# Where two centring products and one evacuation stand in the opening of a layernorm, attention and SwiGLU kernel

## The chip, the cores and the metric

The kernel runs on one core of one Trainium2 chip. The metric is the device time of one execution in microseconds (us), lower is better. Before the change three runs gave 814.28, 814.46 and 814.59 us, with a median of 814.46 us.

## What is computed

The input x has 2048 rows of 1024 values. Each row is normalised, and the normalised rows feed two branches whose results are joined:

```python
xn = _layernorm(x, axis=-1)          # (x - mean) / sqrt(var + eps)
s  = _A_ref(xn, A_wqkv, A_wo)        # 32 heads, window 8, dilation 2, then @ wo
g  = _silu(_B_ref(xn, B_w1, B_w3, B_w2))   # (silu(xn@w1) * (xn@w3)) @ w2
return x + s * g
```

For the change only the opening matters: the mean and the deviation of the first rows of x, and the products of those rows with the q and k parts of wqkv.

## The kernel before, in words

The 2048 rows are worked through in four chunks of 512 rows. For each chunk TensorE computes q, k and v (`qkv`), 14 blocks of gate and up products (`up_block`), the down projection in two halves (`down_half`) and the output projection (`wo_proj`). VectorE's attention work is slipped in beside it by a planner (`Side`) with hand-set costs and due times. Outside the planner the order on every engine is the order in which the code is written: the kernel switches the scheduler off (`tc.manual_schedule()`, line 98). The framework puts in the semaphores for data and for buffers that are used again.

Chunk 0 has no earlier work to hide its layernorm behind, so its opening is written out by hand (lines 511 to 697). Its 512 rows are four tiles of 128 rows, tiles 0 to 3. Tiles 0 and 1 (256 rows, `HC`) go first and by a detour:

- `raw_transpose` (L562) turns the raw tile with TensorE into PSUM, in two banks of four 128x128 blocks each: `b0[0]`, `b0[1]` for tile 0 and `b1[0]`, `b1[1]` for tile 1. The first bank of a tile holds blocks kt 0 to 3 of the 1024 columns, the second kt 4 to 7.
- The row sums become diagonal matrices: `dgs[0]` (L593) from tile 0's sum, and `dgs[1]` from tile 1's two half sums (L594, then L595). `center` (L568) adds a product of ones and this diagonal to a bank, which takes the mean from every row.
- `copy_in` (L574) brings a centred bank to SBUF, into `xcT[:, kt, rows]`, by ScalarE for tile 0 and VectorE for tile 1.
- The products of q and k (`part`, L620) run on `xcT`, centred but not scaled. The factor 1/deviation comes later: `R` holds it (L643, L648, L654), and VectorE multiplies by it on the way out (L291).

After the copies the code issues the statistics of tiles 0 and 1: on ScalarE the squares (L553, L554, L557) and two roots (`std`, L544), on VectorE `stats(1)` (L206 twice, L541), `recip(0, 2)` (L547) and `norm0(0)`, `norm0(1)` (L209). These lines stand ahead of the first `part` call in the code.

The q products go to eight accumulators `banks[0]` to `banks[7]`, one for each column group j, first tile rows 0 to 255. `part(t, kt, js, a, b, ...)` issues one product for each j in `js`, of block kt with columns a to b of the rows. The order is: kt 0 with j 0 to 3 on tile 0 alone (L637), the same on tile 1 (L638), kt 0 with j 4 to 6 on both (L639), kt 1 with j 0 to 6 (L640), then in the loop L641 j = 7 for kt 0 and kt 1, and all eight j for kt 2 to 7.

PSUM has the pools `psum_mm` with six buffers and `psum_aux` with two, one bank each. `psum_aux` first holds `b0[0]` and `b0[1]`, later `banks[4]` and `banks[6]`. `psum_mm` first holds the warm-up target `wps`, `b1[0]` and `b1[1]`, which leaves three free buffers, and later the other six accumulators. `busy(n, w)` (L520) issues n products on constants into `wps`, whose result is not read.

The weights come through SyncE's queue: after four half tiles of x, eight transfers of 256 KB bring the q part of wqkv, one for each kt (L138), then the k part follows with tiles 2 and 3 of x between (L157).

Of the kernel before, what the change touches and what calls it, by code (L numbers as in the profile page):

```python
# [45 lines left out]
def kernel(  # L46
# [12 lines left out]
    P = 128  # L59
# [455 lines left out]
    def one(n):  # L515
        return nc.const_aps.tensor(1.0, (P, n), BF16)

    def busy(n, w=CH):
        for _ in range(n):
            nc.tensor.matmul(wps[:, 0:w], lhsT=one(P), rhs=one(w), start=True, stop=True)  # L520

    V, A = nc.vector.tensor_copy, nc.scalar.copy
# [44 lines left out]
    def center(bank, st, i0=0, n=4):  # L567
        nc.tensor.matmul(  # L568
            bank[:, i0:i0 + n, :], lhsT=ones_b[:], rhs=dgs[st][:].unsqueeze(1).to_broadcast([P, n, P]),
            start=False, stop=True, skip_group_check=True,  # L570
        )

    def copy_in(src, st, k0, n, eng):
        eng(out=xcT[:, k0:k0 + n, st * P:(st + 1) * P], in_=src)  # L574

    b0 = [psum_aux.tile([P, 4, P], FP32, tag="aux", name=f"xt0_{h}") for h in range(2)]
    b1 = [psum_mm.tile([P, 4, P], FP32, tag="mm", name=f"xt1_{h}") for h in range(2)]
# [18 lines left out]
        out=dgs[1][:], in0=ident_d[:], scalar=half1[:, 1:2], in1=dga[:], op0=ALU.mult, op1=ALU.add,  # L596
    )
    center(b0[0], 0)
    busy(2, P)
    center(b1[0], 1, 0, 2)  # L600
    center(b1[0], 1, 2, 2)
    center(b0[1], 0)
    center(b1[1], 1)
    copy_in(b0[0][:, 0:2, :], 0, 0, 2, A)
    copy_in(b0[0][:, 2:4, :], 0, 2, 2, A)
    copy_in(b1[0][:, 0:2, :], 1, 0, 2, V)
    copy_in(b1[0][:, 2:4, :], 1, 2, 2, V)
    copy_in(b0[1][:], 0, 4, 4, A)
    copy_in(b1[1][:], 1, 4, 4, V)

    wq, wk = take_q(0), take_q(1)
    banks = [psum_mm.tile([P, CH], FP32, tag="mm", name="ps_qkv") for _ in range(6)]
# [3 lines left out]
    def part(t, kt, js, a, b, first, src):  # L616

        for j in js:
            o = t * HC + a % HC
            nc.tensor.matmul(  # L620
                banks[j][:, o:o + b - a], lhsT=(wq, wk)[t](kt, j), rhs=src[:, kt, a:b],
                start=first, stop=(kt == KT - 1), skip_group_check=True,
            )
# [9 lines left out]
    for i in range(3):  # L633
        nc.gpsimd.tensor_copy(out=rsb[:, i, :], in_=rs0[:, 0:2] if i == 0 else rest[:])
        if i < 2:
            nc.gpsimd.tensor_sub(rest[:], rs0[:, 0:2] if i == 0 else rest[:], rsb[:, i, :])
    part(0, 0, range(4), 0, P, True, xcT)  # L637
    part(0, 0, range(4), P, HC, False, xcT)  # L638
    part(0, 0, range(4, NJ - 1), 0, HC, True, xcT)  # L639
    part(0, 1, range(NJ - 1), 0, HC, False, xcT)  # L640
# [126 lines left out]
```

## Time and profile before

| What | Value |
|---|---|
| median of three runs | 814.46 us |
| the profiled execution, its own time | 814.30 us |
| span of the profiled execution | 812.5 us |
| TensorE (PE) busy | 804.0 us, 99% of the span |
| VectorE (DVE) busy | 474.7 us, 58% |
| ScalarE (ACT) busy | 188.3 us, 23% |
| GpSimd (POOL) busy | 95.9 us, 12% |
| mean DMA rate over the span | 181 GB/s |
| DMA rate from 6.30 to 10.09 us | 365 GB/s |
| chain that ended last | PE 97% |

All times inside the execution count from the span's start. PE is the matmul side of TensorE and PEld its weight loads, which run beside the matmuls. A timeline row gives start, length, engine, line, operation, output <- inputs, shapes, the number of instructions merged into it, and in brackets the idle time ahead of it with what ended that idle time. [...]

### The profile page before, as it was taken

The numbers are of one execution on the slowest core, as the hardware profiler recorded it, in microseconds if no ns is written. First come the engines' busy times: TensorE is split into PE (matmuls) and PEld (weight loads), VectorE is DVE, ScalarE is ACT, GpSimd is POOL, SyncE is SP. The second block draws the span as 40 slices with busy tenths as digits, with TensorE's granted clock in tenths as the row PEclk, the third lists the DMA queues.
The fourth block names the chain that finished last, engine by engine and source line by source line (L and its number), as shares of the span: only waits on it lengthen the run. The fifth ranks groups of instructions, "written<-read, shape, count | busy, mean of one in ns | idle before, by whom it ended". The sixth has DMA issues, their size and how long they took to land.

```text
span 812.5 us, 9647 instructions
## 1 busy us (share of the span) xinstructions
PE 804.0 (99%) x3827; PEld 411.6 (51%) x3899; DVE 474.7 (58%) x491; ACT 188.3 (23%) x313; POOL 95.9 (12%) x183
## 2 busy tenths in 40 slices
PE   9999999999999999999999999999999999999998
PEld 7954444444665444444466444444446644444444
DVE  5489573962239766495124967559411695649632
ACT  3331241012332133101133213310223321311120
POOL 1000404001100122100010022310001003040010
PEclk9999999999999999999999999999999999999999
DMA  9955989942366698974245769996434487777500
GB/s 282 286 133 156 241 186 256 299 141 74 116 190 170 189 214 212 268 254 144 80 148 135 202 191 210 202 305 213 139 91 156 104 206 191 173 227 241 180 27 26
DMA packets 195069, 147.44 MB, mean 181 GB/s; under 512 B 23536, under 2 KB 175856, under 8 KB 195024
## 3 DMA queue, kind: packets, MB, share of 16 engines
q1 hardware_dynamic: 189440, 134.37, 60.7%
q0 software_dynamic: 5584, 12.46, 6.5%
q8 instruction: 30, 0.49, 0.3%
q14 instruction: 15, 0.12, 0.1%
HBM read 130.02 MB, written 4.19 MB: 165 GB/s over the span
## 4 chain that ended last, share of the span: by engine, by line
PE 97%; DMA 2%; issue 1%; SPq 1%; DVE 0%; DVEq 0%
PE gu L261 47%; PE acc L473 20%; PE ps_qkv L261 17%; PE ps_wo L428 7%; PE ps_qkv L620 3%; PE acc L496 3%; DMA wq<-in_A_wqkv_dram 1%; DMA x_t<-in_A_x_dram 1%; SPq L138 0%; SPq L157 0%; DVE o_t L454 0%; DVE gt L453 0%; SPq L218 0%; PE ps_qkv L648 0%; DVEq L453 0%
## 5 line engine op out<-in xcount | busy, mean ns | idle before, releaser
L261 PE MATMUL gu<-xnT_next,w 128*128 128x512 bf16 x1317 | 289.1, 379 | 1.4
L261 PEld LDWEIGHTS <-w 128*128 128x128 bf16 x1792 | 175.3, 98 | 211.3
L473 PE MATMUL acc<-w,ht 128*128 128x512 bf16 x768 | 169.5, 379 | 0.8
L267 DVE TENSOR_TENSOR ht<-sg,gu 128x512 bf16<-128x512 bf16 x112 | 76.0, 684 | 110.6 <-PE gu L261 88.3
L265 ACT ACTIVATE sg<-gu 128x512 bf16<-128x512 f32 x112 | 66.1, 597 | 269.3 <-PE gu L261 257.8
L261 PE MATMUL ps_qkv<-xnT_next,wq 128*128 128x512 bf16 x565 | 124.2, 379 | 0.6
L473 PEld LDWEIGHTS <-ht 128*128 128x128 bf16 x784 | 76.7, 98 | 92.5
L318 DVE TENSOR_TENSOR prod<-qT,kT 128x4096 bf16<-128x4096 bf16 x32 | 73.1, 2286 | 80.6 <-ACT kT L289 80.6
L261 PEld LDWEIGHTS <-wq 128*128 128x128 bf16 x576 | 82.6, 143 | 41.8
L261 PE MATMUL gu<-xnT,w 128*128 128x512 bf16 x439 | 96.4, 379 | 0.5
L453 DVE TENSOR_TENSOR gt<-gt,s_sb 128x512 f32<-128x512 f32 x31 | 21.4, 690 | 106.1 <-ACT gt L447 69.2
L349 POOL DMA_DIRECT2D L<-E x64 | 37.3, 588 | 282.8 <-DVE E L333 270.8
L402 DVE TENSOR_TENSOR pv<-Pr,vT 128x4096 bf16<-128x4096 bf16 x28 | 63.0, 2285 | 0.0
L329 DVE TENSOR_TENSOR prod<-prod 128x2048 bf16<-128x2048 bf16 x64 | 61.2, 956 | 1.4
L428 PE MATMUL ps_wo<-wo,oT 128*128 128x512 bf16 (+1 forms) x259 | 55.8, 372 | 0.3
L455 POOL DMA_DIRECT2D out_dram<-o_t x31 | 17.0, 548 | 313.3 <-DVE o_t L454 313.3
L447 ACT ACTIVATE gt<-acc 128x512 f32<-128x512 f32 x32 | 19.1, 597 | 150.1 <-PE acc L473 128.4
L391 POOL DMA_DIRECT2D Pr<-pb x64 | 36.8, 582 | 104.4 <-DVE pb L383 97.5
L428 PEld LDWEIGHTS <-oT 128*128 128x128 bf16 x264 | 25.9, 98 | 29.6
L413 DVE TENSOR_TENSOR oT<-oT,pv 128x4096 bf16<-128x4096 bf16 x16 | 36.6, 2290 | 0.4
L440 ACT CAST s_sb<-ps_wo 128x512 bf16<-128x512 f32 x31 | 18.2, 586 | 66.4 <-PE ps_wo L428 65.3
L620 PEld LDWEIGHTS <-wq 128*128 128x128 bf16 x276 | 28.4, 144 | 0.5 <-DMA wq<-in_A_wqkv_dram 0.3
(88 smaller groups left out, 346.1 us busy)
## 6 DMA issues: line engine op xcount, KB each, us to landing
w<-in_B_w_dram SPq DMA_DIRECT2D x168, 512.0 KB, 5.3
wq<-in_A_wqkv_dram SPq DMA_DIRECT2D x36, 512.0 KB, 3.8
wo<-in_A_wo_dram SPq DMA_DIRECT2D x8, 1024.0 KB, 11.7
wq<-in_A_wqkv_dram SPq DMA_DIRECT2D x16, 256.0 KB, 5.7
L<-E POOLq DMA_DIRECT2D x64, 64.0 KB, 6.8
Pr<-pb POOLq DMA_DIRECT2D x64, 64.0 KB, 5.3
xres<-in_A_x_dram SPq DMA_DIRECT2D x4, 1024.0 KB, 6.3
out_dram<-o_t POOLq DMA_DIRECT2D x31, 128.0 KB, 2.0
```

Source lines behind the costliest of these rows:

```text
L261: nc.tensor.matmul(ps, lhsT=lhs(kt), rhs=rhs(kt), start=(kt == 0), stop=(kt == KT - 1))
L265: nc.scalar.activation(out=sg[:], in_=g_ps[:], func=ACTF.Silu)
L267: nc.vector.tensor_mul(ht[:], sg[:], u_ps[:])
L318: nc.vector.tensor_mul(prod, qT[:], kT[:, :, o:o + CH])
L329: nc.vector.tensor_add(prod[:, 0:n, :], prod[:, 0:n, :], prod[:, n:2 * n, :])
L349: nc.gpsimd.dma_start(out=L4[sq * NH:(sq + 1) * NH, r, :, :], in_=E_r[r, :, :, sq * P:(sq + 1) * P],)
L391: nc.gpsimd.dma_start(out=Pr_r[r, :, :, sq * P:(sq + 1) * P], in_=pb[sq * NH:(sq + 1) * NH, :, :],)
L402: nc.vector.tensor_mul(dst, Pr[:, w, :].unsqueeze(1).to_broadcast([P, NJ, CH]), vT[:, :, o:o + CH])
L413: nc.vector.tensor_add(a, a, b)
L428: nc.tensor.matmul(ps[:, 0:w], lhsT=oT[:, j, st * P:(st + 1) * P], rhs=was[dh][:, j, n0:n0 + w], start=(j == 0), stop=(j == NJ - 1),)
L473: nc.tensor.matmul(accs[st][:], lhsT=hts[f][:, st * P:(st + 1) * P], rhs=w2t[:, i, :], start=(f == 0), stop=(f == FT - 1),)
L620: nc.tensor.matmul(banks[j][:, o:o + b - a], lhsT=(wq, wk)[t](kt, j), rhs=src[:, kt, a:b], start=first, stop=(kt == KT - 1), skip_group_ch ...
```

## The change

Three edits, all in the opening:

1. `center(b0[1], 0)`, the second bank of tile 0, moves ahead of the two products on `b1[0]`, to the place of `busy(2, P)`, which goes.
2. `center(b1[1], 1)`, the second bank of tile 1, moves from ahead of the copies to behind the four first products (L637).
3. `copy_in(b1[1][:], 1, 4, 4, V)` moves with it, so that in the code it now stands behind the statistics and the two normalisations as well.

```diff
     center(b0[0], 0)
-    busy(2, P)
+    center(b0[1], 0)
     center(b1[0], 1, 0, 2)
     center(b1[0], 1, 2, 2)
-    center(b0[1], 0)
-    center(b1[1], 1)
     copy_in(b0[0][:, 0:2, :], 0, 0, 2, A)
     copy_in(b0[0][:, 2:4, :], 0, 2, 2, A)
     copy_in(b1[0][:, 0:2, :], 1, 0, 2, V)
     copy_in(b1[0][:, 2:4, :], 1, 2, 2, V)
     copy_in(b0[1][:], 0, 4, 4, A)
-    copy_in(b1[1][:], 1, 4, 4, V)
...
     part(0, 0, range(4), 0, P, True, xcT)
+    center(b1[1], 1)
+    copy_in(b1[1][:], 1, 4, 4, V)
     part(0, 0, range(4), P, HC, False, xcT)
     part(0, 0, range(4, NJ - 1), 0, HC, True, xcT)
     part(0, 1, range(NJ - 1), 0, HC, False, xcT)
```

## The prediction, as it stood before the result

> **What bounds the kernel now.** I read the page's shares first, then the chain that ended last, then PE's waits over the whole span, and last the opening engine by engine. The shares and the chain, from the page:
>
> ```profile
> span 812.5 us, 9647 instructions
> PE 804.0 (99%) x3827; PEld 411.6 (51%) x3899; DVE 474.7 (58%) x491; ACT 188.3 (23%) x313; POOL 95.9 (12%) x183
> ...
> PE 97%; DMA 2%; issue 1%; SPq 1%; DVE 0%; DVEq 0%
> ```
>
> PE is the bound nearly everywhere, so a delay of PE in the opening can only be won back where PE waits later. The waits of PE and of its weight loads over the whole span (columns: total us, times, longest) list just a few, and all lie in the first 11 us. The table of stages agrees: PE is busy 587.15 of the 590 us from 200 to 790. Whatever PE loses in the opening goes to the end.
>
> ```profile
> PEld L620 <- DMA wq<-in_A_wqkv_dram: 0.3, 1, 0.3
> ...
> PE xt L568 <- DVE dg L595: 0.2, 1, 0.2
> PE xt L568 <- DVE dg L593: 0.2, 1, 0.2
> ```
>
> The opening on PE, from its timeline:
>
> ```profile
> 5.00 0.38 PE L568 MATMUL xt<-dg,ones_b 128*128 128x512 bf16 x1 [0.17 <-DVE dg L593]
> 5.22 0.27 PE L520 MATMUL warm_ps<-const-bfloat16-1.0 128*128 128x128 bf16 x2
> 5.66 0.81 PE L568 MATMUL xt<-dg,ones_b 128*128 128x256 bf16 x4 [0.17 <-DVE dg L595]
> 6.31 7.50 PE L620 MATMUL ps_qkv<-xcT,wq 128*128 128x128 bf16 x68
> 13.64 0.49 PE L648 MATMUL ps_qkv<-dgr,ones_b 128*128 128x256 bf16 x3
> ```
>
> The reader is to see 36 of the 68 products run from 6.31, and then a weight load at 10.09 that waited 0.29 us for the transfer of wq. The chain of waits shows that transfer, the one for kt 4:
>
> ```profile
> 4.51 5.54 DMA wq<-in_A_wqkv_dram
> ...
> 10.09 3.71 PE ps_qkv L620 x32
> ```
>
> It is issued at 4.51 and lands at 10.05 whatever PE does. So **before kt 4 there is nothing to win**: products that start sooner only wait longer at 10.09. From there PE runs to 13.64 (32 products, 3.55 us, 0.111 each) and on without a wait. Narrow windows show the starts of the last products before the gap at 9.32, 9.43, 9.54, 9.65 and 9.76: a pace of 0.11. Counting back from 9.76, the last of the 18 products that follow L640 (j = 7 of kt 0 and 1, then kt 2 and 3), j = 7 of kt 0 started at 9.76 - 17 x 0.109 = 7.91.
>
> The other engine that matters is DVE, and one thing about ACT:
>
> ```profile
> 5.25 0.35 DVE L595 SCALAR_TENSOR_TENSOR dg<-ident_d,half,dga 128x128 bf16<-128x128 bf16 x1
> 6.08 1.35 DVE L574 CAST xcT<-xt 128x256 bf16<-128x256 f32 x3 [0.47 <-PE xt L568]
> 7.34 1.28 DVE L206 BATCH_NORM_STATS2 st<-x 128x6 f32<-128x512 bf16 x2
> 8.66 0.21 DVE L541 BATCH_NORM_AGGREGATE mv<-st 128x2 f32<-128x12 f32 x1
> 9.23 0.17 DVE L547 RECIPROCAL rs<-rs 128x2 f32<-128x2 f32 x1 [0.36 <-ACT rs L544]
> 9.43 1.00 DVE L209 TENSOR_SCALAR x<-x,mv,rs 128x1024 bf16<-128x1024 bf16 x2
> ```
>
> ```profile
> 14.98 0.30 ACT L544 ACTIVATE rs<-mv,eps_t 128x1 f32<-128x1 f32 x1 [5.78 <-DVE mv L541]
> 15.19 0.35 ACT L654 COPY R<-ps_qkv 128x256 f32<-128x256 f32 x1
> ```
>
> DVE's rows stand in the order of the code: three copies (starts 6.08, 6.42, 6.75), statistics, reciprocal, two normalisations. The ACT rows show how strict that order is: the copy into R had its products at 14.13 (13.64 + 0.49), and ACT was idle 5.78 us, yet R went behind the root of tile 2 that is written ahead of it. An instruction doesn't overtake one that waits.
>
> **The change part by part.** *First edit.* The two 128x128 fillers (0.11 us of PE) and the later 128x512 `center` change places. That `center` goes from 5.88 to 5.22, and takes 0.22 (5.00 to 5.22 for the first). It fits ahead of 5.66, where PE waits for L595 in any case, so `b1[0]` is centred at 5.66 and 5.77 as before. ACT gets `b0[1]` earlier: its third copy starts after its second instead of at 6.29. Worth on the path: nothing, since these copies feed kt 4 or free `banks[6]`, and nobody waited for either. If the cover of 5.22 to 5.66 failed, the price is 0.22, less the 0.22 gap at kt 4: again nothing.
>
> *Second edit.* The 128x512 `center` on `b1[1]` leaves the place ahead of the first product and stands 4 products behind it: the same 0.22 us on PE before kt 4, so no change in sum. The first product can start at about 6.1 instead of 6.31 (its weights land at 2.61 + 3.4 = 6.01).
>
> *Third edit, the one that counts.* No copy is added, but the 0.68 us copy of `b1[1]` (group row: one 128x512 DVE CAST, 681 ns) is now written behind `recip` and both `norm0`, so on DVE it comes behind L209. What is then behind it, on DVE, is `dgr` (11.04 before, needed at 13.64: covered). Who waits for it on PE: (a) kt 4 of `xcT`, and (b) earlier, the eighth accumulator. `psum_mm` has six buffers. When j = 7 of kt 0 comes, five accumulators (j 0 to 3, 5) hold five, and the sixth is `b1[1]`'s, whose last reader is this copy. That no earlier product waited at 6.5 to 7.4, while `b1[1]` was being read until 7.43, says that j 0 to 6 have other banks. In before the copy ended 0.48 us ahead of its need at 7.91.
>
> Its new time: DVE is free for L206 at 6.75 instead of 7.34, so its chain moves up 0.59. The roots on ACT allow that: `b0[1]`'s copy is 0.34 earlier (5.95 for 6.29), so the first root, 8.29 to 8.58 before, ends at 8.24, and tile 1's variance comes at 8.87 - 0.59 = 8.28. Hence reciprocal 8.64, normalisations 8.84 and 9.30, copy at 9.43 + 2 x 0.46 - 0.59 = 9.76, end 10.44. PE follows a DVE end by 0.06 (4.69 + 0.25 to 5.00; 5.25 + 0.35 to 5.66): j = 7 starts at **10.50** instead of 7.91. Behind it in PE's order stand all products to the end of the span. 18 at 0.11 bring kt 4 to 12.48, its weights long there. 32 more bring L648 to 16.00, against 13.64: **+2.36 us**. The k weights that follow only gain slack; R waits for L648 and is needed later than that by the same shift.
>
> Bounds for the unknown: the shift of 0.59 is at most that (then +2.36) and at least 0 (DVE chain held by ACT: copy at 10.35, +2.95). A faster restart than 0.109 a product isn't in any row; 50 x 0.109 gives +2.31. Below that nothing, unless one of the two waits doesn't exist (rivals). Sum: 814.30 + 2.36 = **816.7 us** against the profiled execution, which lies 0.16 below the median 814.46; own range 816.3 to 817.3.
>
> **The rivals.** *1. Only kt 4 waits.* If j = 7 took a bank that is free, PE would run to kt 4 and wait there for `xcT`: 10.50 for 10.09, +0.41, 814.7. Against it: the count of six buffers.
>
> *2. Not slower.* If the copy ran where DVE first has its input (about 6.9, behind the second copy), ahead of the statistics, it would end near 7.6, ahead of 7.91, and kt 4's landing at 10.05 would decide as before: 814.3, or 814.1 if the 0.21 that the first product gains also ended the 0.22 gap. It decides if the copy ends before about 8.1. Against it: the R copy's row.
>
> *3. PE's clock falls in the stall.* The five 128x512 fillers at the start begin 0.43 apart (1.16, 1.59, 2.01, 2.44), at 5.00 the pace is 0.22: PE starts at half pace and gets up to full after at most 4.2 us of work. The change leaves PE idle from about 7.9 to 10.5, 2.6 us, longer than any idle time in this trace. If that put it back to half pace for as long, it would lose half of 4.2, so +4.5: 818.8. For it: the slow start. Against it: nothing here shows a fall after a stall.
> [...]
>
> *4. The stall comes at an earlier product.* If j = 5 took `b1[1]`'s bank, 9 more products (1.0 us) would stand behind the wait: 817.7. Before's j = 5 at about 6.9 did not wait until 7.43, so I hold this low.
>
> **How the numbers follow.** Forecast 0.76; rival 1 0.07; rival 2 0.05; rival 3 0.07; rival 4 0.05. The range takes in the forecast with its bounds and rivals 3 and 4, with a little below for a shorter copy or an earlier DVE chain: 815.8 to 818.9. What a measurement of this kernel tells from no change is 0.2%, 1.63 us, or 816.09. The forecast and rivals 3 and 4 lie above it, less 0.03 for a stall that is shorter than I count: slower 0.85. Rivals 1 and 2 and that 0.03 lie within, less 0.02 for a gain that no row shows: same 0.13, faster 0.02.
>
> **What would show each step.** Right: DVE's timeline has the 128x512 CAST of L574 behind the two L209 rows, starting near 9.8; PE's L620 has a wait of some 2.6 us with DVE L574 as its releaser, ahead of the 19th product, not the 37th; kt 4 no longer waits for wq; L648 starts near 16.0 and everything after is later by the same 2.3 to 2.4. Wrong: the CAST ahead of L206 (rival 2), a wait of 0.4 to 0.6 us just ahead of the 37th product (rival 1), products 0.21 apart after 10.5 (rival 3), a wait ahead of the 10th product (rival 4). The forecast also falls if a later stage takes the delay back; I find no PE wait that could.

## The result, and the profile after

The changed kernel took 818.21 us in the median of six runs, against 814.45 us for the kernel before in as many: ratio 1.0040, 95% interval 1.0029 to 1.0051. Five of the six lie between 818.19 and 818.74, and one at 816.47. The profiled execution took 818.19 us with a span of 816.4, against 814.30 and 812.5: 3.9 us more span.

The first two lines below are PE's timeline of the changed kernel at the stall, the third the products of the factor R (L648 before, L647 now):

```profile
6.67 1.51 PE L617 MATMUL ps_qkv<-xcT,wq 128*128 128x128 bf16 x14
10.53 7.29 PE L617 MATMUL ps_qkv<-xcT,wq 128*128 128x256 bf16 x50 [2.35 <-DVE xcT L574]
17.65 0.49 PE L647 MATMUL ps_qkv<-dgr,ones_b 128*128 128x256 bf16 x3
```

After 18 products (4 ahead of the centring, 14 behind it) PE stands still for 2.35 us, until a VectorE copy ends, and 50 are left. 50 is 18 + 32, so the wait is ahead of j = 7 of kt 0 and not ahead of kt 4. The R products start 4.01 us later than before (17.65 against 13.64). The copy itself, in VectorE's timeline of the changed kernel:

```profile
8.88 1.00 DVE L209 TENSOR_SCALAR x<-x,mv,rs 128x1024 bf16<-128x1024 bf16 x2
...
9.79 0.69 DVE L574 CAST xcT<-xt 128x512 bf16<-128x512 f32 x1
```

It stands behind the normalisations, ends at 10.48, and PE starts at 10.53. A row's length runs past the next start (in the profile before the 128x512 product at 5.00 is listed with 0.38 us, and the next product starts at 5.22), so a pace is the distance between starts. 50 products at the pace of 0.109 take 5.5 us, but here it is 7.12 (10.53 to 17.65). The table of stages of the changed kernel says why (columns: stretch, its length, busy time and instructions of PE, PEld, DVE, ACT and POOL, then PEclk, the granted clock of PE as a share, DMA share, GB/s):

```profile
8.20:10.50 2.30, 0.00 (x0) 0.00 (x0) 1.90 (x6) 0.39 (x2) 1.25 (x5) 1.00 0.93 331
10.50:10.97 0.47, 0.44 (x5) 0.44 (x5) 0.47 (x1) 0.00 (x0) 0.00 (x0) 1.00 1.07 410
10.97:14.38 3.41, 3.41 (x19) 2.66 (x18) 0.47 (x1) 0.00 (x0) 0.00 (x0) 0.50 0.96 358
14.38:17.65 3.27, 3.27 (x31) 3.26 (x30) 3.09 (x7) 0.30 (x1) 0.00 (x0) 1.00 1.01 354
```

For 3.41 us PE ran at half clock: 19 instructions are listed in that stretch, 31 in the slightly shorter one behind it, and from 11.14 on the products start 0.21 us apart in place of 0.11. So the loss has two parts. Without the slow stretch the R products would start at 10.53 + 50 x 0.109 = 15.98, which is **2.34 us for the stall**; the other 17.65 - 15.98 = **1.67 us** is the clock. Of the 4.01 us 3.9 reach the end; the products from R's line to the first v product take 21.51 us in place of 21.61.

The theory for the experiments: the copy's place in VectorE's queue makes the stall, the stall makes the slow stretch, and nothing else in the change costs or gains. Rivals: the new order on PE itself costs; the slow stretch has another cause; the wait is for another product than j = 7.

### The profile page after: what moved, and what is told of

It is laid out like the page before. It is cut to its first block, busy times and chain, and to the rows that moved or that the text cites. A ratio compares the mean times of both kernels' runs of the same rounds, so it can differ in the third digit from the quotient of the medians.

```text
span 816.4 us, 9643 instructions
## 1 busy us (share of the span) xinstructions
PE 805.6 (99%) x3825; PEld 412.3 (50%) x3897; DVE 474.7 (58%) x491; ACT 188.4 (23%) x313; POOL 95.9 (12%) x183
## 4 chain that ended last, share of the span: by engine, by line
PE 97%; DMA 1%; DVE 1%; issue 1%; SPq 0%; ACT 0%; DVEq 0%
PE gu L261 46%; PE acc L473 20%; PE ps_qkv L261 17%; PE ps_wo L428 7%; PE ps_qkv L617 3%; PE acc L496 3%; DMA x_t<-in_A_x_dram 1%; DMA wq<-in_A_wqkv_dram 0%; DMA x<-in_A_x_dram 0%; DVE xcT L574 0%; DVE st L206 0%; DVE x L209 0%; DVE o_t L454 0%; SPq L157 0%; DVE gt L453 0%
## 5 line engine op out<-in xcount | busy, mean ns | idle before, releaser
L617 PEld LDWEIGHTS <-wq 128*128 128x128 bf16 x276 | 29.3, 145 | 3.7 <-issue 2.5
```

What stands on the lines that cost most here:

```text
L617: nc.tensor.matmul(banks[j][:, o:o + b - a], lhsT=(wq, wk)[t](kt, j), rhs=src[:, kt, a:b], start=first, stop=(kt == KT - 1), skip_group_ch ...
```

## Experiments

Beside each run stands the median of the kernel before on the same chip. A kernel's line numbers shift with its edits: the line of the products is L617 in all profiles shown, that of R L647 to L651.

**Only VectorE's order put right.** The changed kernel, with the moved lines ahead of the statistics:

```diff
+    part(0, 0, range(4), 0, P, True, xcT)
+    center(b1[1], 1)
+    copy_in(b1[1][:], 1, 4, 4, V)
     square0()
...
-    part(0, 0, range(4), 0, P, True, xcT)
-    center(b1[1], 1)
-    copy_in(b1[1][:], 1, 4, 4, V)
     part(0, 0, range(4), P, HC, False, xcT)
```

> The change with one thing different: the four first products, the centring of b1[1] and its copy are written ahead of the statistics instead of behind the normalisations, so that PE's order is that of the change and only the copy's place on VectorE differs. If the loss comes from VectorE's order: copy near 6.9 to 7.6, no wait at j = 7, kt 4 again held by the transfer of its weights near 10.05, full clock throughout, 814.2 to 814.6 us. If it comes from the new order of the products and centrings on PE: still 816 to 818.5.

Measured: 814.52 against 814.48 us, ratio 0.9998 (0.9989 to 1.0007). VectorE and PE in its profile:

```profile
6.08 0.76 DVE L574 CAST xcT<-xt 128x256 bf16<-128x256 f32 x2 [0.49 <-PE xt L568]
7.07 0.69 DVE L574 CAST xcT<-xt 128x512 bf16<-128x512 f32 x1 [0.24 <-PE xt L568]
7.68 1.28 DVE L206 BATCH_NORM_STATS2 st<-x 128x6 f32<-128x512 bf16 x2
```

```profile
6.87 6.97 PE L617 MATMUL ps_qkv<-xcT,wq 128*128 128x128 bf16 x64
13.68 0.49 PE L647 MATMUL ps_qkv<-dgr,ones_b 128*128 128x256 bf16 x3
```

The copy starts at 7.07, the 64 products behind the centring run in one piece, and R's line is at 13.68 against 13.64. The wait for the weights of kt 4 that was expected doesn't show, since here the first product itself waited for weights until 6.36, against a start at 6.31 before. PE's new order makes no difference that these runs can tell (the interval reaches from 0.9 us faster to 0.6 slower), and the loss hangs on the copy's place.

**The first edit alone.** The kernel before, with this:

```diff
     center(b0[0], 0)
-    busy(2, P)
+    center(b0[1], 0)
     center(b1[0], 1, 0, 2)
     center(b1[0], 1, 2, 2)
-    center(b0[1], 0)
```

> The first edit alone: b0[1] is centred in the place of the two fillers, everything else as before. Theory (nothing to win ahead of kt 4): 814.2 to 814.6 us, the first product about 0.2 earlier and the wait for the weights of kt 4 longer by as much. Rival (a shorter way to the first product is worth its length): 814.2 less 0.2, and the wait at kt 4 no longer. If the fillers held the clock up: a stretch at half clock and up to 1.7 us more.

Measured: 814.61 against 814.48 us, ratio 1.0000 (0.9991 to 1.0008): no difference. That the first product comes 0.2 us earlier can't be read from its profile, in which a transfer of x landed late and `b1[0]` was centred at 5.92 instead of 5.66. The wait at kt 4 isn't settled by it either, but R's line is at 13.68 again. No run has a clock below 0.999, so the fillers were not what held the clock up.

**The stall filled.** The changed kernel, with 20 products ahead of j = 7 whose result is overwritten later:

```diff
     part(0, 1, range(NJ - 1), 0, HC, False, xcT)
+    for _ in range(20):
+        nc.tensor.matmul(
+            banks[0][:, HC:CH], lhsT=one(P), rhs=one(HC), start=False, stop=True, skip_group_check=True,
+        )
```

> The change with 20 more products of 128x256 on constants (2.1 us of PE) ahead of j = 7, in the stall, into a half of an accumulator that is overwritten later. The stall stays, PE is busy in it. Theory (the loss is a stall of 2.3 and a stretch of 3.41 us at half clock, 1.7, that the stall brings on): j = 7 still near 10.5, clock 1.00 in every run, 816.5 to 816.9. Rival (the slow stretch has another cause, such as DMA traffic or the products themselves): 818.2 as the change.

Measured: 816.50 against 814.48 us, ratio 1.0025 (1.0016 to 1.0034), 1.7 us less than the change, with *more* work on PE. One slow stretch of 3.41 us at half clock takes the mean clock of a run of 816 us to 0.998. The change's five long runs have this value; the lowest of any run here is 0.999. PE's timeline:

```profile
7.90 2.40 PE L641 MATMUL ps_qkv<-const-bfloat16-1.0 128*128 128x256 bf16 x20
10.49 5.62 PE L617 MATMUL ps_qkv<-xcT,wq 128*128 128x256 bf16 x50 [0.19 <-DVE xcT L574]
15.94 0.49 PE L651 MATMUL ps_qkv<-dgr,ones_b 128*128 128x256 bf16 x3
```

The 50 products start at the same place, 10.49, and now take 5.45 us. That separates the parts: the late copy is worth 2.30 (15.94 against 13.64), the standing still 1.7 more.

**j = 7 put late.** The changed kernel, with the products of j = 7 for kt 0 to 3 behind the others:

```diff
+    for kt in (2, 3):
+        part(0, kt, range(NJ - 1), 0, HC, False, xcT)
     for kt in range(KT):
-        part(0, kt, OPEN if kt > 1 else (NJ - 1,), 0, HC, kt == 0, xcT)
+        part(0, kt, OPEN if kt > 3 else (NJ - 1,), 0, HC, kt == 0, xcT)
```

> The change with the products of j = 7 for kt 0 to 3 put behind all others of kt 2 and 3. If it is the eighth accumulator's bank that waits for the copy: PE goes on until about 9.7, waits there until 10.5, has 4 + 32 products left to L648's line, which then starts near 14.5 instead of 13.64: plus 0.85, 815.3; no fall of the clock after so short a stall. If an earlier product or the first use of tile 1's second half were what waits, the stall stays near 2.4 us and the time 816.7 to 818.2.

> The same kernel as the run with j = 7 put late, for a second profile, since in the first one a transfer of x landed 0.6 us late and PE came to full clock only at 10.2 us. Theory as there: PE works on until about 9.7, waits for the copy until 10.5, L648's line (here L649) near 14.5, 815.3 us. If the bank of j = 7 were not what waits, PE would stand still ahead of the 19th product as in the change.

Measured: 815.41 against 814.48 us, ratio 1.0007 (0.9998 to 1.0016), and in the second set of runs 815.01 against 814.65, ratio 1.0006 (0.9996 to 1.0016). By these times alone it can't be told from no change. The first profile doesn't show the wait: x came late (PE waited 0.57 us for it), PE was at half pace at first (its centring row at 7.21 is 0.63 us long, where the changed kernel's has 0.38), and the 64 products behind the centring stand in one piece; from their start to R's line they take 8.02 us (7.64 to 15.66), against 6.81 in the first experiment (6.87 to 13.68). The second shows the mechanism:

```profile
6.85 2.27 PE L617 MATMUL ps_qkv<-xcT,wq 128*128 128x128 bf16 x21
9.27 0.99 PE L617 MATMUL ps_qkv<-xcT,wq 128*128 128x256 bf16 x7 [0.15 <-DMA wq<-in_A_wqkv_dram]
10.52 4.09 PE L617 MATMUL ps_qkv<-xcT,wq 128*128 128x256 bf16 x36 [0.26 <-DVE xcT L574]
14.45 0.49 PE L649 MATMUL ps_qkv<-dgr,ones_b 128*128 128x256 bf16 x3
```

The copy still ends near 10.5, but now 28 products go ahead of the wait in place of 14, PE waits 0.26 us, and 36 = 4 + 32 are left. R's line is 0.81 later than before, close to the 0.85 expected. It is j = 7 that waits, and no earlier product; and since its first product reads kt 0, which this copy does not write, it waits for the bank and not for data.

**Shorter and longer stalls.** Three kernels put the same copy elsewhere: on ScalarE behind the roots, between the two normalisations, and behind `dgr`.

```diff
-    copy_in(b1[1][:], 1, 4, 4, V)
+    copy_in(b1[1][:], 1, 4, 4, A)
```

> The change with the copy of b1[1] on ScalarE instead of VectorE, behind the two roots (8.00 to 8.64 in the change's trace): copy near 8.65 to 9.25, j = 7 near 9.3, PE idle 1.1 us instead of 2.35. Theory (each later us of j = 7 is a us of the end, less the 0.2 gap at kt 4): L648's line at 9.3 + 5.5 = 14.8, plus 1.15, 815.6; whether the clock falls after 1.1 us is not known from theory, I expect not. Rival (any stall of PE brings on the 3.41 us at half clock): 817.3.

```diff
     norm0(0)
+    part(0, 0, range(4), 0, P, True, xcT)
+    center(b1[1], 1)
+    copy_in(b1[1][:], 1, 4, 4, V)
     norm0(1)
...
-    part(0, 0, range(4), 0, P, True, xcT)
-    center(b1[1], 1)
-    copy_in(b1[1][:], 1, 4, 4, V)
```

> The change with the copy of b1[1] written between the two normalisations: copy at 9.34, its end 10.02, j = 7 at 10.08, PE idle 1.9 us. Stall alone: plus 1.9, 816.4. If the clock falls as after 2.35 us: 818.1. [...]

```diff
     center(b1[1], 1)
+    nc.vector.tensor_mul(
+        dgr[:].rearrange("p i a b -> p (i a) b"), ident[:].unsqueeze(1).to_broadcast([P, 6, P]),
+        rsb[:].rearrange("p i a -> p (i a)").unsqueeze(2).to_broadcast([P, 6, P]),
+    )
     copy_in(b1[1][:], 1, 4, 4, V)
...
-    nc.vector.tensor_mul(
-        dgr[:].rearrange("p i a b -> p (i a) b"), ident[:].unsqueeze(1).to_broadcast([P, 6, P]),
-        rsb[:].rearrange("p i a -> p (i a)").unsqueeze(2).to_broadcast([P, 6, P]),
-    )
```

> The change with the copy of b1[1] written one more place later, behind dgr (10.48 to 11.44 in the change's trace): copy 11.4 to 12.1, j = 7 near 12.2, PE idle about 4 us. Stall: plus 4.0. [...] If the clock stays: 818.5.

PE's timelines of the first and the last of these kernels have the stall in brackets:

```profile
8.99 5.62 PE L617 MATMUL ps_qkv<-xcT,wq 128*128 128x256 bf16 x50 [1.06 <-ACT xcT L574]
...
12.08 7.29 PE L617 MATMUL ps_qkv<-xcT,wq 128*128 128x256 bf16 x50 [3.82 <-DVE xcT L574]
```

| copy | PE idle ahead of j = 7, us | time, us | before, us | ratio (95%) | runs with a mean clock of 0.998 or less |
|---|---|---|---|---|---|
| ScalarE | 1.06 | 815.52 | 814.40 | 1.0013 (1.0004 to 1.0022) | 0 of 11 |
| between the normalisations | 1.97 | 816.76 | 814.40 | 1.0033 (1.0021 to 1.0046) | 2 of 5 |
| behind both (the change) | 2.35 | 818.21 | 814.45 | 1.0040 (1.0029 to 1.0051) | 5 of 6 |
| behind `dgr` | 3.82 | 820.09 | 814.40 | 1.0072 (1.0060 to 1.0085) | 5 of 5 |

The idle times are those of the profiled runs. The times grow with the stall. The clock fell in no run at 1.06 us and in all at 3.82; the shares between (2 of 5, 5 of 6) are of too few runs to be told apart. Of the 60 runs of the kernel before beside the experiments, one has a mean clock of 0.998 (816.63 us). In the kernel with 1.97 us the three runs at full clock took 816.12, 816.63 and 816.76, the two others 817.80 and 817.86. So the change's one run at 816.47, with clock 1.000, is the stall without the fall. The first kernel's median, 815.52, is close to the 815.6 expected. Its profiled run is its fastest (815.00): there the copy began at 8.37, not 8.65, and R's line stands at 14.45, not 14.8. In the second kernel the median, 816.76, is within 0.4 us of the 816.4 expected for the stall alone, and the two runs with the lower clock are within 0.3 us of the 818.1 expected with it. The third, 820.09, lies 1.6 us above the 818.5 expected if the clock stays, which is about the 1.67 us that the slow stretch cost in the change; its 50 products take 7.12 us as there (12.08 to 19.20).

## Why the prediction was right or wrong

**Nothing to win ahead of kt 4: the outcome right, the reason not tested.** With the copy in its old place (first experiment) the new order gave no change in time, though `b0[1]` and `b1[1]` were centred at other places. The reason given, that an earlier start only lengthens the wait at kt 4, was not put to the test: in the profiles of the first two experiments the first product starts at 6.36 and 6.58, no earlier than the 6.31 before.

**The order on VectorE and the bank of j = 7: right, nearly to the step.** Forecast and found: copy at 9.76 and 9.79, its end 10.44 and 10.48, j = 7 at 10.50 and 10.53, 50 products behind the wait. With the stall filled, R's line came at 15.94 against a forecast of 16.00, and the median 816.50 against 816.7 for a sum of 814.30 + 2.36.

**"Against it: nothing here shows a fall after a stall": this is the step that failed.** The clock case had 0.07 and was the common one: 818.21 is 3.76 above before, where the forecast had 2.36. What I had was a trace without any stall longer than the ones at the start, so it said nothing either way, and I took its silence as evidence against. The price of that case was too high: I let the half pace last 4.2 us (2.1 lost), the longest that the slow start allowed. It lasted 3.41 us and cost 1.67, so the case gave 818.2 rather than 818.8. An idle time of 2.35 us was enough for the fall in five runs of six. The range held the result only because it had been drawn to take in this case; the forecast's own range ended at 817.3.

**The rivals.** Only kt 4 waiting (814.7), not slower (814.3) and an earlier product waiting (817.7) are each excluded by the 50 products behind the wait. The second is what the first experiment brings about: 814.52.

## What to carry to other kernels

A copy that frees a buffer holds up the next writer of that buffer (here j = 7, by 2.35 us), so when its lines move in the code, look at what stands ahead of it on its own engine and at the first instruction that needs the buffer, not only at who reads its output. Price a stall of PE twice, once for its length and once for the clock that it may cost; here 1.97 us brought the second part on in two runs of five, and 3.82 in five of five. Where a stall can't be removed, products in it whose result nobody reads kept the clock here (11 runs of 11), and so did real ones brought forward (21 of 21), which also shortened the stall to 0.26 us (j = 7 late).

## What the runs showed of the hardware that was not expected

The clock fell behind a stall, and the two traces that have the fall show 3.41 us at half clock. The trace's own record of the clock has, in the changed kernel, full clock from 4.16 to 10.99, half from 10.99 to 14.40, and full again from there. PE had already started again at 10.53, so the fall came 0.46 us behind the end of the stall. The 3.41 us ahead of the fall:

```profile
7.57:10.98 3.41, 1.06 (x11) 0.93 (x10) 2.97 (x7) 1.02 (x5) 1.25 (x5) 1.00 0.94 331
```

PE was busy 1.06 of 3.41 us in them, 31%; its idle time is the 2.35 us of the stall. In the kernel with the copy between the normalisations, the profiled run kept its clock. Its PE timeline, and two stretches of 3.41 us that meet inside its stall:

```profile
10.63 5.62 PE L617 MATMUL ps_qkv<-xcT,wq 128*128 128x256 bf16 x50 [1.97 <-DVE xcT L574]
```

```profile
6.28:9.69 3.41, 2.33 (x22) 1.96 (x21) 2.58 (x7) 2.85 (x9) 0.19 (x1) 1.00 1.02 316
9.69:13.10 3.41, 2.47 (x23) 2.47 (x23) 2.65 (x5) 0.00 (x0) 1.14 (x4) 1.00 1.05 399
```

The granted clock is 1.00 in both, with PE busy 68% and 72% (2.33 and 2.47 of 3.41). A stretch of the same length that holds the whole stall is busy for 3.41 - 1.97 = 1.44 us at most, 42%. Why the same kernel has the lower clock in two other executions is not shown: for those two runs there is no trace. With the copy behind `dgr` PE was busy 1% of the 3.41 us ahead of the fall (first row), and the slow stretch is at half clock for 3.41 us as well (second row):

```profile
8.71:12.12 3.41, 0.04 (x1) 0.04 (x1) 2.68 (x5) 0.00 (x0) 1.25 (x5) 1.00 1.03 388
```

```profile
12.12:15.53 3.41, 3.41 (x17) 2.72 (x17) 2.66 (x7) 0.30 (x1) 0.00 (x0) 0.50 1.06 394
```

What decides whether the clock falls, and when, these runs don't tell.
